# Layer-3 down-weight gradient as single-bank jobs in the backward stages, and first blocks emitted one stage earlier

## The chip, the cores and the metric

The kernel runs on one core of one Trainium2 chip. Times are device microseconds (us) of that core. Most tables give the median of several executions and the ratio to executions of the kernel before that ran on the same chip. Stage lengths come from one profiled execution of each kernel, so they carry that execution's jitter: the forward part, whose instructions hardly differ between all kernels here, took 284.8 to 286.7 us.

Engines: PE is TensorE, DVE is VectorE, ACT is ScalarE, POOL is GpSimd, SP is SyncE, whose queue issues nearly all loads.

## The reference, cut to what matters

Four layers on 2048 x 512 activations, forward and all gradients: attention without softmax (layers 0 and 2, `A`) and a gated GLU (layers 1 and 3, `B`). Both kinds of layer use one set of weights twice, so each weight gradient is a sum over two layers.

```python
def _B_ref(x, w_gate, w_up, w_down):          # F = 1376
    g = jnp.einsum("bsd,df->bsf", x, w_gate)
    u = jnp.einsum("bsd,df->bsf", x, w_up)
    h = _sigmoid(g) * u
    return jnp.einsum("bsf,fd->bsd", h, w_down)
x = A_x
x = x + _A_ref(_layernorm(x), A_wqkv, A_wo)                    # layer 0
x = x + _B_ref(_layernorm(x), B_w_gate, B_w_up, B_w_down)      # layer 1
x = x + _A_ref(_layernorm(x), A_wqkv, A_wo)                    # layer 2
x = x + _B_ref(_layernorm(x), B_w_gate, B_w_up, B_w_down)      # layer 3
# outputs: x and the gradients of A_x, A_wqkv, A_wo, B_w_gate, B_w_up, B_w_down
```

The gradient of `w_down` is `h.T @ grad`, for layer 3 a 1376 x 512 result summed over 2048 rows. In tiles of 128 x 128 by 128 x 512 that is 11 row chunks times 16 matmuls, 176 in all.

## The kernel before: the parts that the change and the argument touch

After forward, which already contains layer 3's backward ("GLU both"), the backward program runs layer 2's attention in two halves (`a_bwd1`, `a_bwd2`), layer 1's GLU (`b_bwd`), layer 0's attention in two halves, and then a tail with all the weight gradients.

```python
def backward(k):
    k.ps = pool("ps_bwd", 4, space=PSUM)          # four banks "bank"
    k.ps2 = pool("ps_dw", 4, space=PSUM)          # four banks "dwbank"
    k.p_set, k.p_dst = pool("dw_set", 5), pool("dw_stage", 6)
    k.p_sh, k.p_ln = mpool("sh", 2), mpool("lnb", 2)    # two 8 KB buffers: qr_l, sh_t
    # ... cut ...
    a_bwd(k, 2, False)
    b_bwd(k, 1)
    a_bwd(k, 0, True)
    # tail: joint gradients of two layers
    for s in SETS:
        dw_rows(k, "wd", s, [(g3, sv[3]["hhT"]), (g1, sv[1]["hhT"])])
    # ... cut ...

def a_bwd1(k, l, big, ph1, p_dq):                 # first half
    # ... cut ...
    grads(0)                                      # x -> bf16 tile, transposes on PE
    for b in range(NBLK):
        qr = k.p_sh.tile([P, 2, NDC, SB], BF16, name="qr_l", tag="sh")
        nc.sync.dma_start(out=flat(qr), in_=sv["qr"][b])
        # ... cut ...
        for dc in range(NDC):                     # dq_ps -> ACT dq_sb -> DVE u_t (with qr_l)
            # ... cut ...
            if len(late) > 2:
                soft(*late.pop(0))                # t_ps -> DVE w_t -> POOL dqT -> DVE u_t
            if dc == 1 and b + 1 < NBLK:
                grads(b + 1)
        sums(b, g_t, qn)                          # 16 CT_ps matmuls

def a_bwd2(k, l, final, big, pool, CT, dzp):      # second half
    def loads(b):                                 # k.p_h has four 4 KB buffers, tag "h_t"
        dqT = k.p_h.tile([P, NDC, SB], BF16, name="dqT_l", tag="h_t")
        nc.sync.dma_start(out=dqT[:], in_=by_chunk(sv["dqT"], b))
        # ... cut: hT, pkT ...
        hst = k.p_h.tile([P, NB, D], BF16, name="ha_l", tag="h_t")
        nc.sync.dma_start(out=hst[:], in_=by_tile(sv["h"], b * NB, NB))
    def queries(b):
        dh = [k.ps2.tile([P, D], F32, name="dh_ps", tag="dwbank") for _ in range(NB)]
        # ... 16 matmuls on dqT_l ...
```

## Time and profile before

Median 1169.7 us in three executions (1169.7 to 1174.0). The profiled one had a span of 1167.3 us.

These are the first lines of the page of the kernel before, busy time of each engine.

```profile
span 1167.3 us, 15363 instructions
PE 1085.6 (93%) x5439; PEld 508.4 (44%) x5528; DVE 535.8 (46%) x952; ACT 518.1 (44%) x1046; POOL 368.0 (32%) x451
```

The view of windows gives one line for each stage: start and end, length, then busy time and count of PE, PEld, DVE, ACT and POOL, then PE's granted clock (1.00 is full rate), the DMA engines' share and GB/s. The six stretches are layer 2's first and second half, the GLU stage, layer 0's first and second half, and the tail.

```profile
533.50:578.10 44.60, 36.50 (x209) 17.38 (x208) 28.48 (x61) 25.70 (x43) 19.26 (x18) 1.00 0.98 291
578.10:643.80 65.70, 60.02 (x288) 27.59 (x292) 43.00 (x70) 28.92 (x70) 27.39 (x24) 0.97 0.63 198
643.80:767.25 123.45, 115.76 (x518) 51.76 (x528) 64.44 (x93) 53.88 (x120) 23.91 (x17) 0.99 0.74 224
767.25:814.10 46.85, 40.28 (x209) 19.28 (x208) 34.69 (x70) 27.33 (x50) 24.53 (x21) 0.89 0.86 291
814.10:872.60 58.50, 58.09 (x289) 27.25 (x292) 41.95 (x66) 28.05 (x66) 29.97 (x26) 1.00 0.48 169
872.60:1167.00 294.40, 282.87 (x1393) 137.82 (x1415) 6.61 (x12) 34.17 (x73) 35.31 (x58) 1.00 0.90 197
```

Layer 0's second half keeps PE busy throughout. The other five stretches leave PE idle for 6 to 12 us each, and layer 0's first half also ran at a granted clock of 0.89.

The view of waits of PE in the backward stages names the instruction that waited, what it waited for, the sum, the number of times and the longest.

```profile
PE t_ps L889 <- DVE u_t L918: 8.2, 6, 2.5
PE dh_ps L955 <- ACT t_sb L782: 4.1, 2, 3.8
PE dh_ps L818 <- DVE dd_t L839: 3.7, 3, 1.2
PE dq_ps L180 <- ACT gaT_t L878: 3.6, 2, 3.4
PE dh_ps L818 <- ACT dhh_t L837: 3.4, 1, 3.4
```

One of these is dh_ps waiting 3.8 us for ACT t_sb. The timeline of ACT and PE in layer 2's second half shows it.

```profile
626.13 0.67 ACT L782 ACTIVATE t_sb<-dh_ps,rstd 128x512 f32<-128x512 f32 x1
631.78 0.62 ACT L806 CAST g_t<-x 128x512 bf16<-128x512 f32 x1 [4.89 <-DMA gT_t<-g_t]
632.41 0.67 ACT L782 ACTIVATE t_sb<-dh_ps,rstd 128x512 f32<-128x512 f32 x1
633.22 1.02 PE L955 MATMUL dh_ps<-wqkvT,dqT_l 128*128 128x512 bf16 x4 [3.79 <-ACT t_sb L782]
634.59 1.86 PE L955 MATMUL dh_ps<-wqkvT,dqT_l 128*128 128x512 bf16 x4 [0.35 <-ACT t_sb L782]
```

ACT took these instructions in order. The cast into the next stage's gradient tile `g_t` stood still for 4.89 us, behind the transposed load that reads the previous `g_t`. The two t_sb evictions behind it came late, so did the dh_ps banks, and PE stood still.

### The profile page before, as it was taken

The numbers are of one execution on the slowest core, as the hardware profiler recorded it, in microseconds if no ns is written. First come the engines' busy times: TensorE is split into PE (matmuls) and PEld (weight loads), VectorE is DVE, ScalarE is ACT, GpSimd is POOL, SyncE is SP. The second block draws the span as 40 slices with busy tenths as digits, with TensorE's granted clock in tenths as the row PEclk, the third lists the DMA queues.
The fourth block names the chain that finished last, engine by engine and source line by source line (L and its number), as shares of the span: only waits on it lengthen the run. The fifth ranks groups of instructions, "written<-read, shape, count | busy, mean of one in ns | idle before, by whom it ended". The sixth has DMA issues, their size and how long they took to land. (4 is left out here: it accounts for less than half of the span.)

```text
span 1167.3 us, 15363 instructions
## 1 busy us (share of the span) xinstructions
PE 1085.6 (93%) x5439; PEld 508.4 (44%) x5528; DVE 535.8 (46%) x952; ACT 518.1 (44%) x1046; POOL 368.0 (32%) x451
## 2 busy tenths in 40 slices
PE   4978999998899999997998899989999999989997
PEld 2434444444344444443443344444444445634443
DVE  6588744658744445534766555558761000000000
ACT  4468788637645655535435443454462000000120
POOL 6125555302641625231624211135453000000120
PEclk8999999999899999999999999989999999999999
DMA  6987976789995615167964966687639996898885
GB/s 225 252 255 243 237 207 208 228 185 227 279 250 104 181 57 164 63 156 200 320 251 115 257 230 201 201 284 275 217 110 226 266 208 136 214 251 172 194 184 123
DMA packets 376492, 238.01 MB, mean 204 GB/s; under 512 B 287264, under 2 KB 345216, under 8 KB 375392
## 3 DMA queue, kind: packets, MB, share of 16 engines
q1 hardware_dynamic: 362032, 189.93, 63.7%
q0 software_dynamic: 14384, 47.10, 11.7%
q8 instruction: 43, 0.70, 0.3%
q14 instruction: 33, 0.27, 0.1%
HBM read 67.40 MB, written 99.39 MB: 143 GB/s over the span
## 5 line engine op out<-in xcount | busy, mean ns | idle before, releaser
L1094 PE MATMUL dw_ps<-set_t,h_all 128*128 128x512 bf16 (+1 forms) x1007 | 203.9, 362 | 2.2 <-ACT dw_new L1029 1.3
L1094 PEld LDWEIGHTS <-h_all 128*128 128x128 bf16 x1024 | 100.1, 98 | 105.3 <-issue 1.9
L618 POOL TENSOR_TENSOR sd_t<-sd_t,hh_t 128x512 bf16<-128x512 bf16 x88 | 106.6, 1217 | 123.1 <-ACT sd_t L617 52.5
L1029 ACT CAST dw_new<-dw_ps 128x512 bf16<-128x512 f32 (+2 forms) x51 | 25.3, 578 | 250.5 <-issue 160.2
L792 POOL TENSOR_TENSOR x<-t_sb,x 128x512 f32<-128x512 f32 x48 | 71.3, 1496 | 148.9 <-ACT c1n L784 120.5
L1030 POOL DMA_DIRECT2D out_dram<-dw_new x51 | 27.2, 541 | 248.5 <-ACT dw_new L1029 222.8
L782 ACT ACTIVATE t_sb<-dh_ps,rstd 128x512 f32<-128x512 f32 x64 | 43.5, 681 | 124.0 <-PE dh_ps L725 94.9
L180 PE MATMUL g_ps<-hT_t,wg 128*128 128x512 bf16 x352 | 91.4, 382 | 4.5 <-ACT hT_t L283 3.3
L180 PE MATMUL u_ps<-hT_t,wu 128*128 128x512 bf16 x352 | 91.4, 382 | 0.7 <-ACT th_t L614 0.7
L180 PE MATMUL dhh_ps<-gT_t,wdT 128*128 128x512 bf16 x341 | 89.3, 381 | 0.6 <-issue 0.2
L1108 PE MATMUL dw_ps<-g_all,set_t 128*128 128x512 bf16 (+1 forms) x345 | 75.9, 379 | 3.7 <-DMA set_t<-sv_hhT 3.4
L180 PE MATMUL y_ps<-wd,hh_t 128*128 128x512 bf16 x346 | 77.2, 379 | 0.4
L616 DVE SCALAR_TENSOR_TENSOR hh_t<-sd_t,u_ps 128x512 bf16<-128x512 bf16 x88 | 59.9, 681 | 24.9 <-ACT sd_t L615 22.7
L818 PE MATMUL dh_ps<-wuT,dd_t 128*128 128x512 bf16 x167 | 64.4, 385 | 7.2 <-DVE dd_t L839 3.7
L818 PE MATMUL dh_ps<-wgT,dd_t 128*128 128x512 bf16 x174 | 66.9, 385 | 0.5
L615 ACT ACTIVATE sd_t<-th_t,onef 128x512 bf16<-128x512 f32 x88 | 63.4, 721 | 4.6
L617 ACT ACTIVATE sd_t<-th_t,onef 128x512 bf16<-128x512 f32 x88 | 62.4, 709 | 0.0
L839 DVE TENSOR_TENSOR dd_t<-dhh_t,sh_t 128x1024 bf16<-128x1024 bf16 x44 | 32.1, 736 | 54.3 <-ACT dhh_t L837 49.3
L818 PEld LDWEIGHTS <-dd_t 128*128 128x128 bf16 x352 | 34.5, 99 | 50.9 <-DVE dd_t L839 9.1
L697 DVE TENSOR_TENSOR sd_t<-dhh_t,sd_t 128x1024 bf16<-128x1024 bf16 x44 | 32.2, 733 | 53.4 <-POOL sd_t L618 52.1
L892 POOL TENSOR_TENSOR dqT_t<-w_t,qr_l 128x512 bf16<-128x512 bf16 x32 | 37.7, 1188 | 56.4 <-DVE w_t L891 56.0
L180 PEld LDWEIGHTS <-wg 128*128 128x128 bf16 x352 | 34.4, 98 | 46.8 <-issue 6.6
(166 smaller groups left out, 1775.0 us busy)
## 6 DMA issues: line engine op xcount, KB each, us to landing
sv_sd<-sd_t SPq DMA_DIRECT2D x44, 256.0 KB, 2.9
sv_ddT<-sd_t SPq DMA_DIRECT2D x40, 256.0 KB, 2.2
sv_ddT<-dd_t SPq DMA_DIRECT2D x40, 256.0 KB, 4.0
sv_h<-h_t POOLq DMA_DIRECT2D x16, 512.0 KB, 4.7
sv_qr<-pe_t POOLq DMA_DIRECT2D x16, 512.0 KB, 4.7
qr_l<-sv_qr SPq DMA_DIRECT2D x8, 1024.0 KB, 5.8
sh_t<-sv_sd SPq DMA_DIRECT2D x8, 1024.0 KB, 6.9
h_all<-sv_h SPq DMA_DIRECT2D x16, 512.0 KB, 6.6
```

The source lines that it names most:

```text
L180: i = k.nc.tensor.matmul(out, lhsT=lhs(c), rhs=rhs(c), start=(c == 0), stop=(c == n - 1))
L615: nc.scalar.activation(sd[:, 0, :], th[:], ACT.Identity, bias=k.onef[:], scale=-1.0)
L616: nc.vector.scalar_tensor_tensor(hh[:], sd[:, 0, :], 0.5, u_ps[:], ALU.mult, ALU.mult)
L617: nc.scalar.activation(sd[:, 1, :], th[:], ACT.Identity, bias=k.onef[:])
L618: nc.gpsimd.tensor_tensor(sd[:, 1, :], sd[:, 1, :], hh[:], ALU.mult)
L697: k.last_mul = nc.vector.tensor_tensor(dd[:], dhh[:].unsqueeze(1).to_broadcast([P, 2, SB]), dd[:], ALU.mult)
L782: nc.scalar.activation(t_sb[:], dh_ps, ACT.Identity, scale=rstd, accum_out=c1[:])
L792: nc.gpsimd.tensor_tensor(k.xs[st][:], t_sb[:], up, ALU.add)
L818: nc.tensor.matmul(acc[b][j][:], lhsT=dd[:, a, rows(j)], rhs=(k.wuT, k.wgT)[a][:, fc, :], start=(fc == 0 and a == 0), stop=(fc == NFC - 1 ...
L892: nc.gpsimd.tensor_tensor(dqT[:, dc, :], w_t[:], rp[:, dc, :], ALU.mult)
L1094: k.nc.tensor.matmul(ps[ic][:, 0:w], lhsT=h_t[:, ic * P:(ic + 1) * P], rhs=t, start=(i == 0 and st == 0), stop=(i == len(srcs) - 1 and st ...
L1108: k.nc.tensor.matmul(p[0:r, :], lhsT=t[:, f:f + r], rhs=g_t, start=(i == 0 and st == 0), stop=(i == len(srcs) - 1 and st == NST - 1))
```

## The change

Its intent is to take layer 3's 176 matmuls out of the PE-bound tail and to place them in PE's waits in backward, and to emit the first gradient block of each stage in the stage before so that stages start without a gap. To make room, it also rearranges buffers. The diff, cut to its core:

```diff
+class Fill:                       # a generator; each next() emits one matmul
+    def run(self):
+        ahead = self.load(0)      # transposed load of one row chunk of hhT, 512 KB
+        for fc in range(NFC):
+            t, w = ahead
+            ps = k.ps.tile([P, D], F32, name="fill_ps", tag="bank")
+            for st in range(NST):
+                if st == 3 and fc + 1 < NFC:
+                    ahead = self.load(fc + 1)
+                nc.tensor.matmul(ps[0:w, :], lhsT=t[:, st, 0:w], rhs=self.g[st // NB][:, st % NB, :], ...)
+                yield True
+            part = k.p_part.tile([P, D], F32, name="wd_part")
+            nc.scalar.copy(part[0:w, :], ps[0:w, :])
+            k.st.dma_start(out=self.sv["wd"][fc * P:fc * P + w, :], in_=part[0:w, :])
# placing: 12 at the start of an attention first half, 2 for each dc; 4, 8, 8, 16 in a second half;
#          5 or 3 for each of the first chunks of a block in the GLU stage
# early emission
+            if b == NBLK - 1 and fc == 5:
+                k.early = a_grads(k, 0)            # in GLU both; likewise in b_bwd and a_bwd2
-    grads(0)
# buffers
-        k.p_set, k.p_dst = pool("dw_set", 5), pool("dw_stage", 6)
+        k.p_sh = mpool("sh", 2)                    # first, over memory that forward frees early
+        wab = k.p_mt = mpool("wab", 1)
+        k.p_set, k.p_part = mpool("dw_set", 6), mpool("wd_part", 2)
-        if b == 0 and l == 2:                      # transposed loads of wo, wqkv
+        if b == 1 and l == 2:
-        dqT = k.p_h.tile([P, NDC, SB], BF16, name="dqT_l", tag="h_t")
-        nc.sync.dma_start(out=dqT[:], in_=by_chunk(sv["dqT"], b))
+        big, p_dq = pool("ab_big", 1), pool("ab_dq", NBLK)      # dqT stays on chip, 4 tiles
-        dkT = p_dk.tile([P, NDC, SB], BF16, name="dkT_t")
+            dk2.append(k.p_sh.tile([P, 2, NDC, SB], BF16, name="dkT_t", tag="sh"))
# tail
-            dw_rows(k, "wd", s, [(g3, sv[3]["hhT"]), (g1, sv[1]["hhT"])])
+            dw_rows(k, "wd", s, [(g1, sv[1]["hhT"])], sv[3]["wd"])   # adds the fp32 partial sum
```

More of the change, by code (lines that the diff above doesn't have):

```diff
@@ L90 @@
     consts, resid, k.keep = pool("consts", 1), pool("resid", 1), pool("keep", 1)
+    k.small = pool("small", 6)
     k.p_h, k.p_hT = pool("h", 4), pool("hT", 4)
@@ L114 @@
                 d["g"] = k.g_in
+                d["wd"] = dram.tile([F, D], F32, name="sv_wd3")
             else:
@@ L205, in flush_turned, with __init__, load, step @@
         k.nc.sync.dma_start(out=dst, in_=flat(t))
+class Fill:
+    def __init__(self, k):
+        self.k, self.sv = k, k.sv[3]
+        self.g = [k.p_set.tile([P, NB, D], BF16, name="gf_t", tag="set_t") for _ in range(NBLK)]
+        for b in range(NBLK):
+            k.nc.sync.dma_start(out=self.g[b][:], in_=by_tile(k.g_in, b * NB, NB))
+        self.todo = self.run()
+    def load(self, fc):
+        t = self.k.p_set.tile([P, NST, P], BF16, name="hf_t", tag="set_t")
+        w = min(P, F - fc * P)
+        self.k.nc.sync.dma_start_transpose(out=t[:, :, 0:w], in_=self.sv["hhT"][fc * P:fc * P + w, :])
+        return t, w
+    def run(self):
+        k, nc = self.k, self.k.nc
+        ahead = self.load(0)
[5 more added lines that the diff above has]
+                    ahead = self.load(fc + 1)
+                nc.tensor.matmul(ps[0:w, :], lhsT=t[:, st, 0:w], rhs=self.g[st // NB][:, st % NB, :],
+                                 start=(st == 0), stop=(st == NST - 1))
+                yield True
+            part = k.p_part.tile([P, D], F32, name="wd_part")
+            nc.scalar.copy(part[0:w, :], ps[0:w, :])
+            k.st.dma_start(out=self.sv["wd"][fc * P:fc * P + w, :], in_=part[0:w, :])
+    def step(self, n):
+        for _ in range(n):
+            if next(self.todo, None) is None:
+                break
 class LN:
@@ L299, in forward @@
         wf = pool("wfwd", 1)
+        k.p_wa, k.p_t, k.p_dhh = pool("wkvo", 1), pool("th", 2), pool("dhh", 2)
+        wfd = pool("wfwd_d", 1)
         k.ps = pool("ps_fwd", 8, space=PSUM)
-        k.small = pool("small", 6)
         k.sums = {}
@@ L304, in forward @@
         k.wu = wf.tile([P, NDC, F], BF16, name="wu")
-        k.wd = wf.tile([P, NFC, D], BF16, name="wd")
-        k.p_hh, k.p_sd, k.p_t, k.p_dhh = pool("hh", 13), pool("sd", 13), pool("th", 2), pool("dhh", 2)
-        k.p_wa = pool("wkvo", 1)
+        k.wd = wfd.tile([P, NFC, D], BF16, name="wd")
+        k.p_hh, k.p_sd = pool("hh", 13), pool("sd", 13)
         lns = [LN(k, l) for l in range(4)]
@@ L738, in backward @@
         k.ps2 = pool("ps_dw", 4, space=PSUM)
-        k.small = pool("bsmall", 6)
-        k.p_set, k.p_dst = pool("dw_set", 5), pool("dw_stage", 6)
         mctx = ctx.enter_context(ExitStack())
         mpool = lambda name, bufs: mctx.enter_context(tc.tile_pool(name=name, bufs=bufs))
-        k.p_sh, k.p_ln = mpool("sh", 2), mpool("lnb", 2)
-        wab = mpool("wab", 1)
+        k.p_sh = mpool("sh", 2)
+        wab = k.p_mt = mpool("wab", 1)
+        k.p_set, k.p_part = mpool("dw_set", 6), mpool("wd_part", 2)
+        k.p_ln = mpool("lnb", 2)
         k.woT = wab.tile([P, NDC, D], BF16, name="woT")
@@ L748, in backward @@
         k.wdT = w_pool(k, "wdT").tile([P, NDC, F], BF16, name="wdT")
+        k.fill = Fill(k)
         a_bwd(k, 2, False)
@@ L753, in backward @@
         a_bwd(k, 0, True)
+        k.fill.step(NFC * NST)
         h3, h1 = load_all(k, sv[3]["h"], "h_all"), load_all(k, sv[1]["h"], "h_all")
@@ L756, in backward @@
                                      [(h3, sv[3]["ddT"][a]), (h1, sv[1]["ddT"][a])])
+        k.p_dst = mpool("dw_stage", 6)
         joint(0, 0)
@@ L763, in backward @@
         p_all, k.p_all = k.p_all, pool("dw_all_end", 2)
-        g3, g1 = load_all(k, sv[3]["g"], "g_all"), load_all(k, sv[1]["g"], "g_all")
+        g1 = load_all(k, sv[1]["g"], "g_all")
         k.p_all = p_all
@@ L802, in grads @@
         def grads(b):
-            gTs[b] = k.p_hT.tile([P, NB, NDC, P], BF16, name="gT_t", tag="hT_t")
-            g_t = k.p_h.tile([P, NB, D], BF16, name="g_t", tag="h_t")
-            for j in range(NB):
-                nc.scalar.copy(g_t[:, j, :], k.xs[b * NB + j][:])
-                if j % 2:
-                    nc.sync.dma_start_transpose(out=gTs[b][:, j - 1:j + 1].rearrange("p a c q -> p (a c) q"),
-                                                in_=g_t[:, j - 1:j + 1, :].rearrange("p a d -> p (a d)"))
-            k.st.dma_start(out=by_tile(sv["g"], b * NB, NB), in_=g_t[:])
+            gTs[b] = b_grads(k, l, b)
         def back(b, fc, dd):
@@ L824, in back @@
                     ln_bwd(k, l, b * NB + j, acc[b][j][:], hst[:, j, :], k.xs[b * NB + j][:])
-        grads(0)
+        gTs[0] = k.early
         for b in range(NBLK):
+            if b == NBLK - 1:
+                k.early = a_grads(k, 0)
             for f0, nf in FGRP:
@@ L841, in b_bwd @@
                     late.append((b, fc, dd))
+                    if fc < 4 if b == 0 else fc < 3:
+                        k.fill.step(5 if b == 0 else 3)
                     store_dd(k, sv, b, fc, dd, nc.sync)
@@ L853, in a_bwd, with a_grads, b_grads @@
         pool = lambda name, bufs: ctx.enter_context(k.tc.tile_pool(name=f"{name}{l}", bufs=bufs))
-        big = pool("ab_big", 1)
-        with k.tc.tile_pool(name=f"ab_dq{l}", bufs=2) as p_dq, k.tc.tile_pool(name=f"ab_ph1{l}", bufs=2) as ph1:
-            CT, dzp = a_bwd1(k, l, big, ph1, p_dq)
-        a_bwd2(k, l, final, big, pool, CT, dzp)
+        big, p_dq = pool("ab_big", 1), pool("ab_dq", NBLK)
+        with k.tc.tile_pool(name=f"ab_ph1{l}", bufs=2) as ph1:
+            CT, dzp, dqTs = a_bwd1(k, l, big, ph1, p_dq)
+        a_bwd2(k, l, final, big, pool, CT, dzp, dqTs)
+def a_grads(k, b):
+    nc = k.nc
+    g_t = k.p_h.tile([P, NB, D], BF16, name="ga_t", tag="h_t")
+    gT = k.p_hT.tile([P, NB, NDC, P], BF16, name="gaT_t", tag="hT_t")
+    for j in range(NB):
+        nc.scalar.copy(g_t[:, j, :], k.xs[b * NB + j][:])
+        if j % 2 == 0:
+            tp = k.ps.tile([P, 2 * NDC, P], BF16, name="T_ps", tag="bank")
+        for c in range(NDC):
+            nc.tensor.transpose(tp[:, j % 2 * NDC + c, :], g_t[:, j, c * P:(c + 1) * P], k.ident[:])
+        if j % 2:
+            nc.scalar.copy(gT[:, j - 1:j + 1].rearrange("p a c q -> p (a c) q"), tp[:])
+    return g_t, gT
+def b_grads(k, l, b):
+    nc = k.nc
+    gT = k.p_hT.tile([P, NB, NDC, P], BF16, name="gT_t", tag="hT_t")
+    g_t = k.p_h.tile([P, NB, D], BF16, name="g_t", tag="h_t")
+    for j in range(NB):
+        nc.scalar.copy(g_t[:, j, :], k.xs[b * NB + j][:])
+        if j % 2:
+            nc.sync.dma_start_transpose(out=gT[:, j - 1:j + 1].rearrange("p a c q -> p (a c) q"),
+                                        in_=g_t[:, j - 1:j + 1, :].rearrange("p a d -> p (a d)"))
+    k.st.dma_start(out=by_tile(k.sv[l]["g"], b * NB, NB), in_=g_t[:])
+    return gT
 def a_bwd1(k, l, big, ph1, p_dq):
     nc, sv, A = k.nc, k.sv[l], k.A[l]
-    MT = big.tile([P, NDC, D], BF16, name="MT_l")
+    MT = k.p_mt.tile([P, NDC, D], BF16, name="MT_l", tag="MT")
     nc.sync.dma_start(out=flat(MT), in_=sv["MT"][:])
@@ L865, in a_bwd1 @@
     CT_ps = [k.ps2.tile([P, D], F32, name="CT_ps", tag="dwbank") for _ in range(NDC)]
-    late, gs = [], []
-    def grads(b):
-        g_t = k.p_h.tile([P, NB, D], BF16, name="ga_t", tag="h_t")
-        gT = k.p_hT.tile([P, NB, NDC, P], BF16, name="gaT_t", tag="hT_t")
-        for j in range(NB):
-            nc.scalar.copy(g_t[:, j, :], k.xs[b * NB + j][:])
-            if j % 2 == 0:
-                tp = k.ps.tile([P, 2 * NDC, P], BF16, name="T_ps", tag="bank")
-            for c in range(NDC):
-                nc.tensor.transpose(tp[:, j % 2 * NDC + c, :], g_t[:, j, c * P:(c + 1) * P], k.ident[:])
-            if j % 2:
-                nc.scalar.copy(gT[:, j - 1:j + 1].rearrange("p a c q -> p (a c) q"), tp[:])
-        gs.append((g_t, gT))
+    late, gs, dqTs = [], [k.early], []
+    grads = lambda b: gs.append(a_grads(k, b))
     def sums(b, g_t, qn):
@@ L896, in soft @@
             k.st.dma_start(out=by_chunk(sv["dqT"], b), in_=dqT[:])
-    grads(0)
+    k.fill.step(12)
     for b in range(NBLK):
@@ L911, in a_bwd1 @@
         dqT = p_dq.tile([P, NDC, SB], BF16, name="dqT_t")
+        dqTs.append(dqT)
         for dc in range(NDC):
@@ L919, in a_bwd1 @@
             late.append((b, dc, dq, u_t, qp, rp, dqT))
+            k.fill.step(2)
             if len(late) > 2:
@@ L932, in a_bwd1, with a_bwd2 @@
     k.st.dma_start(out=sv["CT"][:].rearrange("(c p) d -> p c d", p=P), in_=CT[:])
-    return CT, dzp
-def a_bwd2(k, l, final, big, pool, CT, dzp):
+    return CT, dzp, dqTs
+def a_bwd2(k, l, final, big, pool, CT, dzp, dqTs):
     nc, sv = k.nc, k.sv[l]
-    p_dk, p_dph, p_o = pool("ab_dk", 2), pool("ab_dph", 1), pool("ab_o", 1)
+    p_dph, p_o = pool("ab_dph", 1), pool("ab_o", 1)
     def loads(b):
-        dqT = k.p_h.tile([P, NDC, SB], BF16, name="dqT_l", tag="h_t")
-        nc.sync.dma_start(out=dqT[:], in_=by_chunk(sv["dqT"], b))
         hT = k.p_hT.tile([P, NB, NDC, P], BF16, name="haT_l", tag="hT_t")
@@ L948, in loads @@
         nc.sync.dma_start(out=hst[:], in_=by_tile(sv["h"], b * NB, NB))
-        return hT, pkT, dqT, hst
+        return hT, pkT, hst
     def queries(b):
@@ L954, in queries @@
             for c in range(NDC):
-                nc.tensor.matmul(dh[j][:], lhsT=ld[b][2][:, c, rows(j)], rhs=k.wqkvT[:, c, :], start=(c == 0), stop=False)
+                nc.tensor.matmul(dh[j][:], lhsT=dqTs[b][:, c, rows(j)], rhs=k.wqkvT[:, c, :], start=(c == 0), stop=False)
         return dh
@@ L961, in keys @@
         nc.vector.tensor_scalar(dph[:], pkT[:], -EPS, 1.0, ALU.add, ALU.min)
-        dkT = p_dk.tile([P, NDC, SB], BF16, name="dkT_t")
+        if b % 2 == 0:
+            dk2.append(k.p_sh.tile([P, 2, NDC, SB], BF16, name="dkT_t", tag="sh"))
+        dkT = dk2[b // 2][:, b % 2]
         for dc in range(NDC):
@@ L968, in keys @@
                                            dph[:, :, dc, :], ALU.add, ALU.mult)
-        k.st.dma_start(out=by_chunk(sv["dkT"], b), in_=dkT[:])
+        k.st.dma_start(out=by_chunk(sv["dkT"], b), in_=dkT)
         return dkT
-    ld = [loads(0)]
+    ld, dk2 = [loads(0)], []
     mask4 = k.bdmask[:].unsqueeze(1).to_broadcast([P, NDC, P])
@@ L980, in a_bwd2 @@
     dh = queries(0)
-    Wp = big.tile([P, NDC, D], BF16, name="Wp_t")
+    k.fill.step(4)
+    Wp = k.p_mt.tile([P, NDC, D], BF16, name="Wp_t", tag="MT")
     Nv = big.tile([P, NDC, D], BF16, name="Nv_t")
@@ L1001, in a_bwd2 @@
             dks.append(keys(b + 1))
-        hT, pkT, dqT, hst = ld[b]
+        hT, pkT, hst = ld[b]
         dkT = dks[b]
         if b:
+            if b == NBLK - 1 and not final:
+                k.early = b_grads(k, 1, 0)
+            k.fill.step(8 if b + 1 < NBLK else 16)
             dh = queries(b)
@@ L1097, in dw_cols, with dw_rows @@
         put(k, ps[ic][:, 0:w], nm, rows(ic), slice(base + c0, base + c0 + w))
-def dw_rows(k, nm, cols, srcs):
+def dw_rows(k, nm, cols, srcs, part):
     c0, w = cols
@@ L1110, in dw_rows @@
     for p, (f, r) in zip(ps, fs):
-        put(k, p[0:r, :], nm, slice(c0 + f, c0 + f + r), slice(0, D))
+        t = k.p_sm.tile([P, D], F32, name="part_l", bufs=4)
+        k.nc.sync.dma_start(out=t[0:r, :], in_=part[c0 + f:c0 + f + r, :])
+        new = k.p_dst.tile([P, D], BF16, name="dw_new")
+        k.nc.vector.tensor_tensor(new[0:r, :], p[0:r, :], t[0:r, :], ALU.add)
+        k.st.dma_start(out=k.outs[nm][c0 + f:c0 + f + r, :], in_=new[0:r, :])
 _INS = ['A_x', 'A_wqkv', 'A_wo', 'B_x', 'B_w_gate', 'B_w_up', 'B_w_down', 'grad_out']
```

## The prediction

> **What bounds it now.** TensorE. The page gives PE busy 93% of a 1167.3 us span. In the timeline warm 128x512 matmuls start every 0.216 us (16 chunks of a group in 3.45 us), which agrees with the Trainium skill, "TensorE: Matmul & The Clock Gate", "Wait — 56ns, not 53.3ns?" (215.7 ns). I price matmuls at that and call the rest of a stage slack (estimates from the timeline's starts):
>
> - layer-2 attention backward, first half: 534.4 to 578.1 = 43.7 us for 34.6 us of work: slack 9.1
> - its second half: 578.1 to 643.8 = 65.7 for 57.9: slack 7.8
> - layer-1 GLU backward: 643.8 to 767.3 = 123.4 for 113.9: slack 9.5
> - layer-0 attention, first half: 767.3 to 814.2 = 46.9 for 34.6: slack 12.3; second half 0.6
> - weight-gradient tail: 872.7 to 1167.3 = 294.6 for about 283: slack 11
>
> The waits name the slack: t_ps after DVE u_t, itself after qr_l loads (8.2 us); dh_ps after ACT t_sb (4.1); first dq_ps after ACT gaT_t (3.6); first dh_ps after ACT dhh_t (3.4, a chain that began with the transpose of gT_t); three 1.25 us waits at GLU block boundaries. After such gaps matmuls start every 0.43 us for some 4 us; the windows show a granted clock of 0.88 in layer 0's first half. That is the half-rate state of the same skill page ("What's actually happening").
>
> **What the change does.** It moves 176 matmuls (11 row chunks x 16), 38.0 us, from the tail into backward: 44 in each attention first half, 36 and 5 in the second halves, 47 in the GLU stage. Backward slack is 39.3 us, so the counts fit almost exactly. Emitting the next stage's first gradients earlier removes the 3.4 us starts, and dqT stays on chip (eight 512 KB loads gone). It adds 11 transposed 512 KB loads, 11 ACT copies of about 0.58 us, an fp32 round trip of 2.8 MB each way and 11 DVE adds; these engines are half busy. It takes one of four PSUM banks.
>
> **How much arrives.** PE executes in order, so a fill only pays where PE would have waited. I expect residual slack of 3 us (layer 2 first half), 2 (second half), 2.5 (GLU), 5 in layer 0 (qr_l still takes 6 to 8.6 us to land after its buffer frees). Backward then ends at about 884: 11 us later, with 38 us more work. The tail loses 38 us, but it is close to DMA-bound too: DMA share is 1.11 in 1020 to 1060, where PE already waited 3.4 us for set_t. The h2/h0 loads and partial sums now fall into half the time, so I give back 2 to 4 us. Net: 38 - 11 - 3 = 24 to 28 us.
>
> **Prediction: 1143 us, 80% range 1130 to 1156.** Faster by over 2%: 0.60; within 2%: 0.38; slower: 0.02.
>
> **What would show it.** PE busy time about unchanged (1085 us); layer 0's tail starting at 880 to 888 and lasting 255 to 262 us; granted clock in layer 0's first half above 0.95; the waits dq_ps after gaT_t and dh_ps after dhh_t gone; wait t_ps after u_t reduced from 8.2 to below 4; wait for set_t in the tail 3 to 8 us; forward to 534 us unchanged.
>
> **What would make it wrong.** (a) Three banks are too few: dq_ps and T_ps wait on DVE w_t; then about 1155. (b) DMA: its share is 1.00 in layer 2's first half already; extra transposes delay qr_l. (c) The compressed down-weight phase of the tail starves on set_t by 10 us. (d) Better: nearly all 39 us is filled; then about 1132.

## More of the kernel before

The two first halves and the GLU stage start with `grads(0)`, which casts and transposes block 0 of x as the `ln_bwd` calls of the stage before left it. In `b_bwd` its tile is `g_t`, also of tag `h_t`. The view of waits of PE in the backward stages names five waits.

## The result, and the profile after

| | before | changed |
|---|---|---|
| median, us | 1171.85 (4 runs, 1169.7 to 1175.1) | 1158.01 (4 runs, 1154.0 to 1159.2) |
| ratio of means | | 0.9874, 95% interval 0.9838 to 0.9910 |

Ratios here and below are the mean time of one kernel's runs over the mean of the other's runs of the same rounds, so not quite the ratio of the medians quoted. The change gains 1.3%. The prediction was 1143 us, with a range of 1130 to 1156 and a gain of over 2% at 0.60; 1158.0 us was measured. The profiled execution of the changed kernel, span 1152.2 us, was the fastest of the four.

First lines of the page of the changed kernel:

```profile
span 1152.2 us, 15422 instructions
PE 1083.4 (94%) x5434; PEld 507.3 (44%) x5528; DVE 539.9 (47%) x963; ACT 519.4 (45%) x1046; POOL 377.6 (33%) x462
```

The same six stretches in the view of windows of the changed kernel:

```profile
536.30:585.50 49.20, 45.72 (x233) 21.48 (x236) 26.47 (x62) 25.00 (x43) 20.95 (x19) 0.97 0.78 229
585.50:653.30 67.80, 66.18 (x323) 30.76 (x328) 42.93 (x70) 32.09 (x77) 29.59 (x27) 1.00 0.78 200
653.30:782.40 129.10, 125.08 (x580) 56.74 (x591) 63.29 (x91) 56.41 (x121) 25.68 (x19) 1.00 0.75 222
782.40:834.00 51.60, 46.46 (x238) 22.08 (x240) 33.76 (x71) 27.36 (x51) 27.25 (x24) 0.97 1.03 310
834.00:895.30 61.30, 59.38 (x289) 27.43 (x293) 41.89 (x66) 27.55 (x66) 30.67 (x27) 1.00 0.56 162
895.30:1152.20 256.90, 245.42 (x1220) 120.09 (x1239) 14.31 (x23) 28.95 (x62) 35.98 (x59) 1.00 0.92 204
```

The tail is 37.5 us shorter, nearly all of the 38.0 us of matmuls taken out of it. The backward stages together are 20 us longer (339 to 359), where I had expected 11.

PE's waits in the backward stages of the changed kernel:

```profile
PE dq_ps L182 <- ACT dq_sb L976: 5.1, 3, 2.2
PE dh_ps L856 <- DVE dd_t L879: 3.4, 4, 1.6
PE T_ps L911 <- ACT dq_sb L976: 1.7, 1, 1.7
PE dpk_ps L182 <- DVE dkT_t L1027: 1.1, 1, 1.1
PE dh_ps L1014 <- ACT t_sb L827: 0.9, 2, 0.6
```

Most of the waits that I had named are gone or small, in particular t_ps behind u_t (8.2 us) and dh_ps behind t_sb (from 4.1 us to 0.9); those of dh_ps behind dd_t stay (3.7 and 3.4 us). New ones, dq_ps and T_ps behind dq_sb, have come. From these two traces alone one would say: the fills went into the waits, and a part of them did not fit. That reading is wrong, as the experiments show.

### The profile page after: what moved, and what is told of

It reads as the page before. It is cut to its first block, busy times and chain, and to the rows that moved or that the text cites. A ratio compares the mean times of both kernels' runs of the same rounds, so it can differ in the third digit from the quotient of the medians. Undisturbed runs are those within 1.5% of the kernel's fastest.

```text
span 1152.2 us, 15422 instructions
## 1 busy us (share of the span) xinstructions
PE 1083.4 (94%) x5434; PEld 507.3 (44%) x5528; DVE 539.9 (47%) x963; ACT 519.4 (45%) x1046; POOL 377.6 (33%) x462
## 4 chain that ended last, share of the span: by engine, by line
PE 39%; DVE 4%; issue 4%; DMA 3%; ACT 3%; POOL 1%; SPq 1%; POOLq 0%; DVEq 0%; ACTq 0%
PE dw_ps L1159 15%; PE dh_ps L856 5%; PE dh_ps L1075 3%; PE dhh_ps L182 2%; DVE junk L831 2%; PE dw_ps L1173 2%; PE CT_ps L943 2%; PE fill_ps L238 2%; PE dq_ps L182 2%; PE dh_ps L767 2%; DVE t_sb L832 2%; PE dh_ps L1014 2%; DMA qr_l<-sv_qr 1%; PE dpk_ps L182 1%; POOL x L837 1%
## 5 line engine op out<-in xcount | busy, mean ns | idle before, releaser
L1094 ACT CAST dw_new<-dw_ps 128x512 bf16<-128x512 f32 (+1 forms) x40 | 19.5, 573 | 214.5 <-PE dw_ps L1159 150.0
L1179 DVE TENSOR_TENSOR dw_new<-dw_ps,part_l 128x512 bf16<-128x512 f32 (+1 forms) x11 | 6.9, 684 | 176.0 <-PE dw_ps L1173 164.6
L1095 POOL DMA_DIRECT2D out_dram<-dw_new x40 | 21.5, 543 | 168.0 <-ACT dw_new L1094 166.3
L654 ACT ACTIVATE th_t<-g_ps 128x512 f32<-128x512 f32 x88 | 51.3, 589 | 7.6 <-PE g_ps L182 7.4
```

The costliest lines, as they stand in the source:

```text
L654: nc.scalar.activation(th[:], g_ps[:], ACT.Tanh, scale=-0.5)
```

## The experiments

Stage lengths of all profiled runs, worked out from the starts of the stages' first and last matmuls in the timeline (so they differ by up to 0.6 us from windows with rounded edges). "Fill" counts the fill matmuls in the five stages, 0.216 us each. "Backward" is the time from the end of GLU both to the last backward matmul.

| run | what | fill | L2 first | L2 second | GLU | L0 first | L0 second | backward | median | ratio to before |
|---|---|---|---|---|---|---|---|---|---|---|
| before | | 0 | 44.6 | 65.7 | 123.6 | 46.8 | 58.7 | 339.3 | 1171.9 | 1 |
| changed | | 176 | 49.2 | 67.8 | 129.3 | 51.1 | 61.8 | 359.2 | 1158.0 | 0.9874 |
| e1 | fills in a lump at the end | 0 | 37.4 | 58.5 | 127.2 | 41.5 | 58.6 | 323.2 | 1185.8 | 1.0113 |
| e2 | e1, a bank held | 0 | 37.6 | 58.5 | 127.2 | 43.3 | 58.6 | 325.2 | 1185.4 | 1.0119 |
| e3 | no early emission | 176 | 49.1 | 68.1 | 129.5 | 50.3 | 69.5 | 366.6 | 1157.1 | 0.9870 |
| e4 | fill loads once | 176 | 45.6 | 67.8 | 129.7 | 49.6 | 68.3 | 360.9 | 1155.0 | 0.9848 |
| e5 | no fill | 0 | 38.2 | 58.5 | 124.8 | 41.6 | 58.6 | 321.6 | 1158.7 | 0.9910 |
| e6 | no fill, no early emission | 0 | 39.8 | 58.5 | 124.0 | 45.0 | 58.6 | 325.8 | 1156.9 | 0.9886 |
| e7 | halved buffers | 176 | 45.6 | 67.8 | 128.2 | 47.4 | 65.9 | 354.9 | 1152.7 | 0.9843 |
| e8 | 64 fills, GLU only | 64 | 38.4 | 58.5 | 131.2 | 42.7 | 58.6 | 329.4 | 1151.7 | 0.9846 |
| e9 | e6, dqT loaded again | 0 | 41.1 | 64.4 | 123.7 | 45.0 | 58.6 | 332.8 | 1163.9 | 0.9930 |
| e10 | e6, wo and wqkv early | 0 | 39.5 | 58.5 | 125.0 | 43.8 | 58.6 | 325.3 | 1155.5 | 0.9875 |
| e11 | e6, old pools | 0 | 39.8 | 58.5 | 124.2 | 45.1 | 58.6 | 326.1 | 1159.2 | 0.9889 |
| e12 | e7 and e8 | 64 | 36.6 | 58.5 | 131.6 | 41.5 | 58.6 | 326.8 | 1143.6 | 0.9775 |
| e13 | before, dqT on chip | 0 | 42.4 | 58.5 | 127.4 | 44.1 | 58.6 | 331.0 | 1158.0 | 0.9896 |
| e14 | e9, own buffers for dqT | 0 | 39.9 | 63.0 | 125.6 | 43.6 | 64.4 | 336.5 | 1166.1 | 0.9961 |
| e15 | e5, halved buffers | 0 | 36.4 | 58.5 | 128.8 | 42.3 | 58.6 | 324.6 | 1151.4 | 0.9841 |

The 95% intervals of the ratios have half-widths of 0.0030 to 0.0060 (3.5 to 7 us). All results were correct except e4's.

### What was in question

After the result I had three theories for the missing 9 us of backward: theory Q (the fills stand in the loop that frees a qr_l buffer), theory B (the fill takes one PSUM bank too many) and theory D (the fill's loads compete for DMA).

### e1: no fill inside backward

```diff
     def step(self, n):
+        if n < NFC * NST:
+            return
         for _ in range(n):
...
-        k.fill.step(NFC * NST)
+        k.fill.step(NFC * NST + 1)
```

> The changed kernel, but no gradient job runs inside the backward stages: all 176 fill matmuls run in one lump after the last backward stage. What stays is the early emission, dqT kept on chip and the new pools. Backward (end of the GLU-both stage to the first fill matmul) took 339 us before and 359 us in the changed kernel with 38 us of fill in it. Theory Q (the layer halves are paced by the two qr_l buffers: a buffer frees late and its load takes 6 to 8 us): about 328 us here, and PE still waits in both attention first halves for DVE u_t on qr_l, 5 us or more in sum. Theory B (the fill's PSUM bank is what costs): about 321 us, because all four banks are free and the waits of dq_ps and T_ps on ACT dq_sb are gone. Total: the lump has only two load buffers, so 45 to 55 us for 38 us of matmuls: 1165 to 1180 us.

Backward took 323.2 us, between the two. The waits of t_ps on qr_l were below 1 us each in layer 2's first half and up to 2.1 us in layer 0's. The time was worse than expected, 1185.8 us, because PE waits for transposed loads in the lump (14.2 us in five waits). But the weighty finding is one that I had not asked for. Without any fill, backward is already 16 us shorter than before (339.3 to 323.2), and layer 2's second half has no wait left: 58.5 us for an estimated 57.9 us of work. So these waits were not filled. Something else in the change had removed them.

### e2: a bank held idle

```diff
         k.fill = Fill(k)
+        hold = k.ps.tile([P, D], F32, name="hold_ps", tag="bank")
+        nc.vector.memset(hold[0:1, 0:1], 0.0)
...
+        nc.vector.memset(hold[0:1, 0:1], 0.0)
         k.fill.step(NFC * NST + 1)
```

> As e1, but one PSUM bank of the four is held idle from the start of backward until the lump, as the fill holds it in the changed kernel. Theory B (three banks are too few): backward 6 us or more longer than in e1, with dq_ps and T_ps waiting on ACT dq_sb or DVE w_t for 5 us or more. Theory Q: within 2 us of e1.

Backward was 2.0 us longer than e1's, and the time the same. Theory B falls: three banks are enough where no fills run. That a bank matters in the presence of fills is not tested by this.

### e3: no early emission, fills kept

```diff
-            if b == NBLK - 1 and fc == 5:
-                k.early = a_grads(k, 0)
-        gTs[0] = k.early
+        gTs[0] = b_grads(k, l, 0)
-    late, gs, dqTs = [], [k.early], []
+    late, gs, dqTs = [], [a_grads(k, 0)], []
# and the two other early calls taken out
```

> The changed kernel with the fills spread as they are, but the first gradient block of each stage emitted at the start of its own stage again. If early emission is a real part of the gain: 5 to 8 us slower than the changed kernel (first dq_ps waits for gaT_t, first dh_ps for dhh_t after the transpose of gT_t, each near 3.4 us less the fill that now stands there). If the fills alone cover those gaps: within 2 us.

1157.1 us, ratio 0.9870 against 0.9874. With the fills there, early emission gains nothing.

This run's profile shows a cost that the fills brought. The tail's first transposed loads are now issued in layer 0's second half. In the timeline of SP and PE of e3:

```profile
835.45 19.63 SPq L1134 DMA_TRANSPOSE set_t<-sv_ddT  x3
855.17 0.53 SPq L999 DMA_DIRECT2D haT_l<-sv_hT  x1
859.10 6.12 PE L182 MATMUL dpk_ps<-haT_l,Wp_t 128*128 128x512 bf16 x14 [6.71 <-DMA haT_l<-sv_hT]
```

Three transposed loads kept the SP queue for 19.6 us, the load of haT_l stood behind them, and PE waited 6.7 us. The same wait is 0.6 us in the changed kernel's profile, 5.2 in e4 and 3.7 in e7. It is absent in all profiles with no fill, or fill in the GLU stage only, where this stage takes 58.6 us (apart from e14, which has waits of its own).

### e4: the fill loads its operand once (wrong result)

```diff
-                    ahead = self.load(fc + 1)
+                    ahead = (t, min(P, F - (fc + 1) * P))
```

> The changed kernel with wrong results on purpose: the fill loads its transposed operand once instead of 11 times and reuses it, so 10 transposed 512 KB loads are missing and PE does the same matmuls. Theory D (the fill's loads take DMA time from qr_l): the layer-0 first half, 51.6 us, gets 3 us or more shorter and the kernel 4 us or more faster. Theories Q and B: the first halves stay within 1.5 us, the kernel within 3 us.

The ratio was 0.9848 against 0.9874, 3 us, which is within the noise. Layer 2's first half was 3.6 us shorter, layer 0's only 1.5, and layer 0's second half 6.4 us longer, mostly by the wait just shown. So the fill's loads may cost some 5 us in the two first halves (one profile each), but theory D's marks, 3 us in layer 0's first half and 4 us in the kernel, were not reached. The edit also takes ten transposed loads out of the SP queue, so it does not tell DMA time from queue time.

### e5: no fill at all

The layer-3 gradient goes back into the tail, as in the kernel before. Everything else of the change stays.

```diff
-        k.fill = Fill(k)              # and every k.fill.step(...)
-            dw_rows(k, "wd", s, [(g1, sv[1]["hhT"])], sv[3]["wd"])
+            dw_rows(k, "wd", s, [(g3, sv[3]["hhT"]), (g1, sv[1]["hhT"])])
```

> The changed kernel without the gradient jobs: the layer-3 down-weight gradient is computed in the tail together with layer 1's, as before; early emission, dqT on chip and the new pools stay. e1 showed backward of 323 us with no fill in it, against 339 before and 359 with 38 us of fill. Theory R (the fills only move 38 us of matmuls and absorb next to no waiting; the gain comes from the rest): backward 321 to 326 us, tail 291 to 297, profiled span 1148 to 1158, timed within 4 us of the changed kernel. Rival F (the spreading is what gains): 1165 or more.

1158.7 us against 1158.0 of the changed kernel; by the ratios e5 is 4 us slower, within the noise. The part that names the change gains nothing that these runs can resolve. The view of windows of e5, the same six stretches:

```profile
534.70:572.90 38.20, 35.05 (x193) 16.48 (x192) 30.21 (x61) 23.89 (x41) 19.24 (x18) 1.00 0.71 234
572.90:631.40 58.50, 58.11 (x289) 27.31 (x294) 41.42 (x69) 28.94 (x70) 28.28 (x24) 1.00 0.69 195
631.40:756.20 124.80, 116.70 (x535) 52.77 (x545) 65.02 (x93) 56.39 (x122) 23.92 (x17) 0.99 0.77 225
756.20:797.70 41.50, 35.13 (x192) 16.56 (x191) 38.77 (x69) 25.37 (x48) 25.22 (x22) 1.00 0.92 309
797.70:856.20 58.50, 58.11 (x289) 27.27 (x294) 42.34 (x68) 27.72 (x65) 30.00 (x26) 1.00 0.40 136
856.20:1153.80 297.60, 285.54 (x1393) 138.55 (x1415) 7.42 (x12) 34.51 (x73) 35.81 (x58) 0.98 0.88 193
```

Set against the changed kernel, the fills lengthen the five stages by 11.0, 9.3, 4.5, 9.5 and 3.2 us, 37.5 us together (table: changed minus e5), for 9.5, 7.8, 10.1, 9.5 and 1.1 us of matmuls, 38.0 us. They absorbed 0.5 us of waiting in sum. Only in the GLU stage did they absorb some, 5.6 us, and the other stages gave 5.1 us of that back.

Not all waits had been removed, though. Three of those that I had named are still there in e5:

```profile
PE t_ps L944 <- DVE u_t L973: 4.5, 5, 2.1
PE dh_ps L854 <- DVE dd_t L877: 3.7, 3, 1.2
PE dh_ps L854 <- ACT dhh_t L875: 3.7, 1, 3.7
```

The first and the last are gone from the changed kernel's view, so the fills did take their place; but the attention halves grew by the whole of their fill all the same, and only the GLU stage gained from it.

### e6: no fill and no early emission

The edits of e3 and e5 together.

> As e5, and the first block of each stage emitted at the start of its own stage. Together with the changed kernel, e3 and e5 it makes a table of two by two. If early emission and fills cover the same gaps (e3: with fills, early emission was worth nothing): without fills it is worth 5 to 9 us, so this is 5 to 9 us slower than e5, near 1163. If dqT on chip and the pools are the whole gain: within 2 us of e5.

My expectation failed. 1156.9 us is not slower than e5. So the table of two by two is flat: 1158.0 with both, 1157.1 with fills alone, 1158.7 with early emission alone, 1156.9 with neither (ratios 0.9874, 0.9870, 0.9910 and 0.9886). Neither of the two things in the change's name gains anything measurable. Early emission does shorten layer 0's first half in the profile (45.0 to 41.6 us), but e5 has 1.5 us more in GLU both, which now contains the first block's work, and 0.8 us more in the GLU stage; what is left does not show in the times.

### e7: halved buffers

The two 8 KB buffers of `p_sh` become four of 4 KB. The tiles in them are loaded and freed by halves.

```diff
-FGRP = [(0, 4), (4, 4), (8, 3)]
+FGRP = [(0, 2), (2, 2), (4, 2), (6, 2), (8, 2), (10, 1)]
-        k.p_sh = mpool("sh", 2)
+        k.p_sh = mpool("sh", 4)
-        qr = k.p_sh.tile([P, 2, NDC, SB], BF16, name="qr_l", tag="sh")
+        for d2 in range(2):
+            qr = k.p_sh.tile([P, 2, 2, SB], BF16, name="qr_l", tag="sh")   # half of the columns
```

> The changed kernel with the two 8 KB buffers of p_sh cut into four of 4 KB: qr_l, sh_t and dkT_t are loaded and released by halves, same bytes. Theory Q (fills stand in the loop that frees a qr_l buffer, so they delay the next qr_l by what they fill): the waits of dq_ps on ACT dq_sb behind qr_l in the last block (2.1 us each, with half-rate matmuls after them) go, both attention first halves shrink by 2 to 4 us each, the kernel is 4 to 8 us faster than the changed one. If the first halves are paced by ACT and DVE at their start instead: within 2 us.

Both first halves shrank, by 3.6 and 3.7 us, and the wait in the last block is gone. The median is 5.3 us below the changed kernel's, by the ratios 3.6 us, which is within the noise. The stages support theory Q. Without fills the same edit (e15 against e5) shortens layer 2's first half by 1.8 us and leaves layer 0's as it is within 1 us, so it is the fills that had made the qr_l buffers matter more. In the timeline of PE of the changed kernel one sees what the late qr_l costs:

```profile
573.17 1.03 PE L182 MATMUL dq_ps<-gaT_t,MT_l 128*128 128x512 bf16 x4
577.13 1.66 PE L182 MATMUL dq_ps<-gaT_t,MT_l 128*128 128x512 bf16 x4 [2.07 <-ACT dq_sb L976]
```

After a wait of 2.07 us the same four matmuls take 1.66 us and not 1.03, so PE ran slower after the gap as well. A fill matmul stood right behind the waiting one and did not pass it: PE took its matmuls in order.

### e8: fills in the GLU stage only

```diff
-        for fc in range(NFC):
+        for fc in range(4):                       # 4 of 11 row chunks
-                    if fc < 4 if b == 0 else fc < 3:
+                    if fc < 4 if b == 0 else fc < 5:
# k.fill.step(...) taken out of a_bwd1 and a_bwd2; the other 7 chunks stay in the tail
```

> Fills only where they were seen to absorb waiting: e1 against the changed kernel shows the GLU backward growing by 2.1 us for 10.1 us of fill, the attention stages by as much as their fill. Here 4 of the 11 row chunks (64 matmuls, 13.8 us) are filled in, all in the GLU stage; the other 7 stay in the tail as before. Theory R: GLU stage 130 to 134 us, attention stages as in e1 (37, 58, 42, 59 us), so 6 to 9 us faster than e5 and than the changed kernel. Rival (e1's long GLU stage was chance): same as e5.

The GLU stage took 131.2 us for 13.8 us more work than in e5 (124.8), so 7.4 us of waiting was filled, and the kernel is 7.0 us faster than e5. Here the idea of the change works. With the two 8 KB buffers these runs show it nowhere else (for the halved buffers see e7 against e15 below).

### e9: dqT loaded from memory again

From e6, one more piece undone.

```diff
+        dqT = k.p_h.tile([P, NDC, SB], BF16, name="dqT_l", tag="h_t")
+        nc.sync.dma_start(out=dqT[:], in_=by_chunk(sv["dqT"], b))
-                nc.tensor.matmul(dh[j][:], lhsT=dqTs[b][:, c, rows(j)], ...)
+                nc.tensor.matmul(dh[j][:], lhsT=ld[b][3][:, c, rows(j)], ...)
```

> From e6 (no fills, no early emission; still 13 us faster than before) one more piece is undone: the second attention halves load dqT from DRAM again into the h_t buffers, eight 512 KB loads. Theory H (keeping dqT on chip is what emptied the second half of layer 2: before 65.7 us, e6 58.5): the second half takes 62 us or more, the wait of dh_ps on ACT t_sb (3.8 us before) or dpk_ps on dkT_t returns, the kernel is 4 to 8 us slower than e6. Rival P (the new order of pools did it): within 2 us of e6, second half below 60.

As theory H said: layer 2's second half took 64.4 us (e6 58.5), and the kernel was 7.0 us slower (1163.9 against 1156.9; by the ratios 5.2, with half-widths of 4 to 5). The old chain came back with its old numbers. From the waits and the timeline of e9:

```profile
PE dh_ps L1006 <- ACT t_sb L823: 4.1, 2, 3.7
626.81 0.62 ACT L914 CAST g_t<-x 128x512 bf16<-128x512 f32 x1 [4.84 <-DMA gT_t<-g_t]
```

And the same cast in e6, where dqT_l takes no `h_t` buffer. It waited 2.09 us, at a time when no eviction of dh_ps stood behind it, and no wait of PE of 0.5 us or more is in this stage:

```profile
609.36 0.19 ACT L825 ACTIVATE c1n<-c 128x1 f32<-128x1 f32 x1
611.64 1.14 ACT L914 CAST g_t<-x 128x512 bf16<-128x512 f32 x2 [2.09 <-DMA gT_t<-g_t]
612.68 0.72 ACT L832 ACTIVATE t_sb<-t_sb,c1n 128x512 f32<-128x512 f32 x1
```

Two more numbers of e9 belong here. Layer 0's second half, which loads dqT in the same way but has no GLU stage and so no `g_t` after it, took 58.6 us with the four loads as without them. And e9 as a whole is still faster than the kernel before, 0.9930 (0.9891 to 0.9969): some 8 us of the gain do not need dqT on chip.

### e10 and e11: the loads of wo and wqkv early again, and the old pools

Both start from e6. e10 is one line, `if b == 0 and l == 2`; e11 restores the order of the SBUF pools in forward and backward.

> From e6, the transposed loads of wo and wqkv are issued in block 0 of layer 2 again and not in block 1. If this deferral is what shortened the first half of layer 2 (44.6 us before, 39.8 in e6): 42 us or more here and 2 to 5 us slower than e6. If the new pools did it (qr_l and MT_l land in memory that is free earlier): within 1.5 us of e6.

> From e6, the order of the SBUF pools of before in forward and backward: the buffers of qr_l, MT_l and the weights lie again over memory that the forward stage frees last. Theory P: first half of layer 2 43 us or more (e6 39.8), the first qr_l load issued after 530 us and not near 510, kernel 3 to 6 us slower than e6; second halves stay at 58.5. Rival: no change.

Neither changed the time by more than the noise (1155.5 and 1159.2 against 1156.9), and layer 2's first half stayed at 39.5 and 39.8 us. My expectation for e11 failed: with the old pools the first qr_l load still went out at 515 us in the SP timeline, where it had gone out at 537 in the kernel before.

### e12: e7 and e8 together

> e7 and e8 together, the version that the runs point to: four 4 KB buffers in place of two of 8 KB, and only four row chunks filled in, all in the GLU stage. e7 gained about 5 us on the changed kernel, e8 about 6. If they add up: 1145 to 1149 us, GLU stage 128 to 131 us, layer-0 first half 39 to 42 us, 2% faster than before or close to it. If halving the buffers only helps where fills stand in the attention halves: as e8, 1150 to 1153.

1143.6 us (six runs, 1142.8 to 1151.7), ratio 0.9775, interval 0.9737 to 0.9813: 2.3% faster than before (1.9 to 2.6%) and faster than the changed kernel. Its stages in the view of windows, GLU and layer 0's first half:

```profile
630.40:762.00 131.60, 129.39 (x610) 58.59 (x609) 64.76 (x93) 58.80 (x126) 27.61 (x22) 1.00 0.86 245
762.00:803.50 41.50, 36.57 (x193) 16.88 (x192) 37.54 (x69) 25.30 (x48) 25.93 (x22) 0.96 0.83 283
```

PE is busy for 129.4 of 131.6 us in the GLU stage.

### e13: the kernel before with dqT on chip

The edits of e10 and e11 together. Apart from helper functions and unused declarations, this is the kernel before with four dqT tiles kept, and with dkT, MT_l and Wp in shared buffers to make room for them.

> e10 and e11 undone together: old pools and early wo/wqkv loads. This is the kernel before with two things from the change: dqT stays on chip, and dkT, MT_l and Wp sit in shared buffers to make room. Theory H1 (dqT on chip is nearly the whole gain): 1156 to 1162, first half of layer 2 near 40 us as in e10 and e11, second half 58.5. Theory H2 (pools or deferral, either suffices for the first half): first half back to 43.5 to 45 us, second half 58.5, kernel 1160 to 1165, 4 to 5 us slower than e10 and e11.

1158.0 us, ratio 0.9896 (0.9852 to 0.9940): within noise of the changed kernel. The second half is at 58.5 us. The first half, 42.4 us, lies between the two expectations. Keeping dqT on chip, with the sharing that makes room, gives the whole gain within what these runs can resolve. What the sharing gives without dqT on chip was not run; e9, which has the sharing too, says that dqT alone need not be all of it.

### e14: dqT loaded again, into buffers of its own

```diff
-        dqT = k.p_h.tile([P, NDC, SB], BF16, name="dqT_l", tag="h_t")
+        dqT = p_dql.tile([P, NDC, SB], BF16, name="dqT_l")
```

> As e9, dqT loaded from DRAM again, but into two buffers of its own and not into the four h_t buffers. If the eight loads cost (bytes, latency): as e9, second half of layer 2 near 64 us, 1164. If what cost was the h_t buffer that dqT_l takes from the GLU's gradient tile g_t: second half below 60 us, the wait of dh_ps on ACT t_sb gone, 1156 to 1159 like e6.

This came out between the theories. The wait of dh_ps on ACT t_sb is gone, as the buffer theory says. But the stage takes 63.0 us all the same, with new waits (2.5 us of Wp_ps on DVE dkvT, 0.6 us of dh_ps on the load of dqT_l), and the kernel takes 1166.1 us. The first dqT_l load was issued 8.0 us after the stage began (579.8 against 571.8), where in e9 it went out 12 us before. So this edit gave the load a new lateness of its own, and it doesn't cleanly separate the buffer from the loads. What speaks for the buffer is e9's layer 0, where the loads into `h_t` cost nothing (58.6 us).

### e15: halved buffers without fills

> The changed kernel with no gradient jobs at all and with the four half buffers: e12 without its 64 fill matmuls. If the halves alone give e12's gain: 1143 to 1147. If the fills in the GLU stage carry their 6 us also here: 1149 to 1154.

1151.4 us, so e12's 64 fills are worth 7.8 us (1151.4 to 1143.6), as in e8 against e5 (7.0). The halved buffers are worth 7.3 us without fills (e5 to e15) and 8.1 with them (e8 to e12). Their place is not settled by the profiles: e15's profiled run was its slowest, and its GLU stage of 128.8 us is the longest of the runs without fills.

## Why the prediction was wrong, point by point

- **Where PE had slack before: right.** The stage lengths and the count of 39.3 us stand, and without fills 16 to 18 us of it is gone (e1, e5).
- **The tail: length right, start late.** Predicted were 255 to 262 us and a start at 880 to 888; it took 256.9 and started at 895, as backward had grown by more than I thought. The loss of 38 us arrived, and the feared starving on set_t was 2.9 us in the view of waits.
- **"dqT stays on chip (eight 512 KB loads gone)": priced at nothing, and the largest gain that these runs can place.** The prediction lists it among the details and gives it no time. By e9 it is worth 5 to 7 us, 5.9 of them in layer 2's second half, and by e13 it gives, together with the sharing that makes room, about 12 us (1.04% of 1169 us by the ratio; the medians, 1168.9 and 1158.0, differ by 10.9), all of the gain within noise. These 12 us and the 8 us that e9 gains without it come to more than the 13 us of e6, so the division between dqT, the sharing and the new pools stays open.
- **"A fill only pays where PE would have waited": this step failed, with the residual slack of 3, 2, 2.5 and 5 us that followed from it.** The sum built on it was 38 us of fill for 11 us of longer backward; the fills alone made the five stages 37.5 us longer (changed against e5). It assumed that the waits of the kernel before would still be there for the fills, and that a fill put into a stage with waits takes them up. Neither held. First, some 16 us of the slack were gone: with the rest of the change alone (e5) the second halves have under 1 us of slack and layer 2's first half 4.5 us (38.2 for an estimated 33.7 of work; the early block's 16 transposes are not in it). Secondly, of the estimated 24 us that e5 still leaves, about 10 in the GLU stage, 8 in layer 0's first half and 4.5 in layer 2's, the fills took up only the 5.6 in the GLU stage. Into the four attention halves 129 of the 176 fills (44, 36, 44 and 5), 27.9 us by 0.216 us each, were placed, and they lengthened these stages by 33.0 us (11.0, 9.3, 9.5, 3.2). Backward grew by 20 us and not by 11. As a sum over the two profiles: I expected +11 in backward and -35 in the tail; the spans show +2.8 before backward (533.5 to 536.3, where GLU both now holds the next first block), +20 in backward and -37.5 in the tail. The profiled execution was also the fastest of the changed kernel's, 4 us below its median.
- **"Emitting the next stage's first gradients earlier removes the 3.4 us starts": no measurable part of the time.** e3 against the changed kernel, and e6 against e5.
- **Risk (a), three banks: not shown.** e2 costs 2.0 us of backward with no fills. Risk (b), DMA: 3 us by the ratios, within the noise (e4). Risk (d) did not occur.
- **The signs to look for were poor.** I wrote that the waits named would shrink if the fills worked. They shrank, in part for another reason (e1, e6), and where the fills did remove them (t_ps behind u_t from 4.5 us in e5 to nothing) the stages still grew by the whole fill. A wait that has gone doesn't say what removed it, nor that time was gained.

Why fills in the attention first halves absorb nothing is only partly shown. By e7, some 3.6 us in each can be put down to qr_l buffers that are freed late, but in layer 2 half of that is there without fills too (1.8 us, e15 against e5). In layer 2's first half, even with halved buffers, 9.5 us of fill costs 9.2 us (e7 against e15), as there is little waiting left to fill (36.4 us for 33.7 of work). In layer 0's it costs 5.1 us. A second cost is not removed by e7: the wait for haT_l in layer 0's second half, 0.6, 6.7, 5.2 and 3.7 us in the four profiles with 176 spread fills (changed, e3, e4, e7). The changed kernel's profile, its fastest run, has the least of it.

What stays open: how the 5 to 7 us of e9 divide between the loads and the `h_t` buffer (e14 is unclear), and why layer 2's first half fell from 44.6 us to 42.4 in e13 and to 39.5 to 39.8 in e6, e10 and e11, where either the pools or the deferral are new or both are. A single profile of each with a jitter of 1 to 2 us doesn't settle the second.

The Trainium skill, "Perfetto Trace Analysis", "Optimization Strategy", says that consistent bubbles on an engine that should be saturated can mean that there isn't enough SBUF or PSUM for the next tile. This case shows one such gap and not a repeated one: 3.79 us of PE idle time began at a tile that waited for its buffer, on ACT, two steps away from PE.

## What to carry to other kernels

Before you price a change by the waits that it will fill, ask for each wait whether another part of the same change removes it; then test the named part alone, by taking out nothing else. Filling a wait with other work paid here in the GLU stage (7 us for 13.8 us of matmuls). It cost its full price where no wait was left (the second halves), and in the first halves, where e7 suggests that the fill stood ahead of the instructions that free the next buffer. Follow a wait back to its first cause: a 3.8 us wait of PE on an eviction was an in-order engine standing at a cast for a buffer, and keeping on chip the tile whose reload had held buffers of that pool gained 5 to 7 us (e9 against e6), where moving 38 us of matmuls gained nothing that could be resolved.

## What the Trainium skill lacked or had wrong

- "TensorE: Matmul & The Clock Gate", "Why this matters for your kernels", advises against PE-idle gaps above about 3 us. The advice does not say that shorter gaps are safe, and the traces have no such limit: in the changed kernel four matmuls after a wait of 2.07 us took 1.66 us, four before it 1.03, while in the kernel before the matmuls after a wait of 2.44 us (at 553.55) started every 0.216 us as before it. After the wait of 3.79 us (at 633.22) the first four took 1.02 us and only the next four 1.86.
- "DMA: Bandwidth & Descriptors", "Issuing engines are not separate DMA queues", says that the sequencer's time to initiate a DMA is usually small relative to the DMA. For transposed loads it was not: three of them held the SP queue for 19.6 us (e3), 8.2, 6.4 and 4.8 us, and their data landed 5.7, 5.3 and 2.0 us after that, while a plain load took the queue for 0.5 us. A plain load behind them made PE wait 6.7 us. Other transposed loads of this kind took the queue for less (three in 7.0 us at 900.32); why these took longer is not shown.
- No page read says that a fill placed in an in-order queue can delay the release of the buffer that the queue waits for next. Halving that buffer took 3.6 and 3.7 us from the two stages (e7).
